# Attention and feed-forward in one kernel: value products and sums grouped on quarters of the array's columns, first transfers reordered

## The chip, the cores and the metric

The kernel runs on one core of one Trainium2 chip. A core has a matrix engine (TensorE, PE in the profile), three engines for elementwise work (VectorE, DVE; ScalarE, ACT; GpSimd, POOL) and a queue that issues transfers (SyncE, SP). The metric is the device time of one execution in microseconds. Comparisons use the median of several runs.

## The reference

Four batches of 448 tokens, 12 heads of 64. Attention with a soft cap, then a feed-forward block over all 1792 tokens (768 to 2048 to 768) with a squared ReLU:

```python
scores = q @ k.T / sqrt(64)
scores = cap * tanh(scores / cap)
attn = exp(scores - max(scores)); attn = attn / (sum(attn) + 1e-9)
x = (attn @ v)                      # heads side by side: [1792, 768]
h = x @ w_in                        # [1792, 2048]
g = s * max(h, 0) ** 2 + b
out = g @ w_out                     # [1792, 768]
```

The data have 64-bit inputs, which the kernel reads as pairs of 32-bit words and converts itself (weights: 512 KB per piece of 128 x 512).

## The kernel before, in words

**Attention.** The 12 heads of a batch are worked in 6 pairs (24 pairs in all). For a pair, `load` (L376) transfers keys, queries and values. `scores` (L387) makes the transposed scores in four calls: c = 0, 1, 2 take 128 keys each, and two matmuls, one per head, run beside each other on the two halves of the array's rows (L402); c = 3 takes the 64 keys that are left of both heads, in one matmul on the full array (L398). Each is fp32, which the chip runs as two passes, so a call of two matmuls stands in the trace as x4, and one as x2. ACT then applies tanh (L409) and exp (L413). The score PSUM has two buffers.

`pv` (L453) makes what comes after: `value(c)` multiplies the exps by the values, for c < 3 with one matmul per head on halves of the array's columns (L466), for c = 3 with one matmul on the full array (L462). `total` sums the exps over the keys by matmuls with ones, on quarters of the columns (L474): the first call takes c = 0 and 1, the second c = 2 and 3. Each of the six calls is an operation of its own for PE. The result (one PSUM buffer, `ps_v`) is copied to `pw` (L482 on ACT or L483 on DVE); the sums go through small transfers to be inverted and spread (`normal`, L417), POOL multiplies (`num`, L336), and after six pairs a batch is scaled and split into a high and a low fp16 half (`x`).

**Feed-forward.** `m1` (L711) makes one block of 128 of the 2048 columns for a batch: 18 fp16 matmuls (high x high, high x low, low x high; L722 to L724), then ReLU (L732), square (L737), high half (L325) and low half (L335 or L336) into `gt`. `m2` (L750) makes one block of 128 output columns: 48 fp16 matmuls (L768 to L770) in four operations of 12, then scaling (L788) and the transfer out. The weights are converted on the chip in `win` (L565) and `wout` (L628): sign and exponent work on DVE and POOL, squares for a norm (L579), then high and low halves.

**What sets the order.** Every operation is recorded in a `Plan` (L20) with a duration, a rank and what it reads and writes. `emit` (L67) simulates the engines: at each step every engine offers, of its operations in order of rank, the first that can start at once, or else the one that can start first, and the earliest of all is taken. The chip then runs exactly this order on each queue. `CHOICE` (L204) holds the ranks (`spans`), the engines that may take each kind of work, and the number of buffers. On SP, transfers without dependencies go out by rank: before, the ranks of the first weight piece, the scalars (-13 to -11) and the first keys and queries (-12) lie close together. Ahead of all stands a warm-up of 11 matmuls on zeros (L833).

Of the kernel before, what the change touches and what calls it, by code (L numbers as in the profile page):

```python
# [7 lines left out]
F32 = mybir.dt.float32  # L8
# [5 lines left out]
ALU = mybir.AluOpType  # L14
# [5 lines left out]
class Plan:  # L20
# [32 lines left out]
                found[k] = True  # L53
        return list(found)

    def op(self, eng, dur, rank, fn, r=(), w=(), move=0.0, port=False, late=0.0):
        self.any({eng: (dur, fn)}, rank, r, w, move, port, late)

    def any(self, ways, rank, r=(), w=(), move=0.0, port=False, late=0.0):

        self.ops.append((ways, rank, tuple(r), tuple(w), move))
        self.more.append((port, late))

    def emit(self):  # L67
        n = len(self.ops)
# [30 lines left out]
        busy = {}  # L99
# [9 lines left out]
        before = {"PE": 0.14, "POOL": 0.02}  # L109
        shy = CHOICE["shy"]  # L110
        cold = 0.0

        def when(i, eng):
            ways, _, r, w, _ = self.ops[i]
# [31 lines left out]
        while todo:  # L146
            best = None
            for reach in (80, n):
                for e, q in queue.items():
                    pick = None  # L150
                    for i in q[:reach]:
                        t = when(i, e)
                        if t is not None and (pick is None or t < pick[0] - 1e-6):
                            pick = (t, i)
                            if t <= busy[e]:
                                break
                    if pick and (best is None or pick[0] < best[0]):
# [12 lines left out]
            for k in self.base((*r, *w)):  # L170
                if k not in held:
                    p = self.make[k][0]
                    held.add(k)
                    slot[k] = head[p] % len(free[p])
                    free[p][slot[k]] = None
                    head[p] += 1
            if e == "PE":
                if t - busy[e] > 3.0:
                    cold = t + 4.0
                if t < cold:  # L180
                    dur += min(dur, (cold - t) / 2)
# [20 lines left out]


CHOICE = {  # L204
    'bias': 6,
    'shy': {'DVE': 0.3, 'POOL': 0.5},
    'spans': {
        ('a', 0): (-2.0, 64.9),
        'w': (-8.6, 102.1),
        ('m1', 0): (65.4, 102.7),  # L210
        'o': (97.1, 180.8),
        ('m2', 0): (93.5, 201.5),
        ('a', 1): (112.5, 186.2),
        ('m1', 1): (199.3, 288.6),
        ('m2', 1): (275.5, 309.7),
        ('a', 2): (151.1, 242.3),
        ('m1', 2): (111.6, 298.4),
        ('m2', 2): (278.3, 336.0),
        ('a', 3): (286.2, 308.4),
        ('m1', 3): (421.3, 519.9),  # L220
        ('m2', 3): (346.0, 349.0),
    },
    'alias': 2,
    'direct': 6,
    'cslag': 13,
    'late': 0.5,
    'warm': 11,
    'pvo': 0.52,
    'pair': 0.85,
    'evac': ('ACT', 'DVE'),  # L230
    'sq': ('ACT', 'DVE'),
    'expo': ('POOL',),
    'whi': ('DVE', 'POOL'),
    'ohi': ('DVE', 'POOL'),
    'xhi': ('ACT', 'DVE', 'POOL'),
    'xmul': ('POOL',),
    'relu': ('ACT', 'DVE'),
    'gsq': ('ACT', 'DVE'),
    'glo': ('DVE', 'POOL'),
    'ghi': ('ACT',),  # L240
    'cs': ('DVE', 'POOL'),
    'slots': (
        ('w', 7), ('kraw', 3), ('qraw', 3), ('vp', 3), ('t', 2), ('ph', 3), ('pt', 2), ('rd', 3), ('pw', 3),
        ('num', 11), ('cmp', 3), ('x', 6), ('r', 2), ('sq', 5), ('o', 2), ('cs', 2),
    ),
}

# [2 lines left out]
def attention_moe_kernel(  # L250
# [123 lines left out]


    def load(bb, c2, rank, vrank):  # L376
        kr = buf(("k", bb, c2), "kraw", [128, SK], F32)
        dma(262144, rank - 10, lambda: nc.sync.dma_start(P[kr], kT[bb, c2]), w=[kr])
        kq = buf(("q", bb, c2), "qraw", [128, S], F32)
        dma(229376, rank - 10, lambda: nc.sync.dma_start(P[kq], qT[bb, c2]), w=[kq])  # L380
        kv = buf(("v", bb, c2), "vp", [128, NC + 1, 2 * D], F32)
        dma(
            262144, vrank - 10,
            lambda: nc.sync.dma_start(P[kv].rearrange("p a d -> p (a d)"), v2[bb * NP + c2]), w=[kv],
        )

    def scores(bb, c2, c, rank):  # L387

        kr, kq = ("k", bb, c2), ("q", bb, c2)
        kp = buf(("sc", bb, c2, c), "ps_s", [128, 2, 512], F32)  # L390
        kt = buf(("t", bb, c2, c), "t", [128, 2, S], F32)
        last = c == NC
        kh = buf(("ph", bb, c2, c), "pt" if last else "ph", [128, S] if last else [128, 2, S], F32)

        def mm():
            ps, k, q = P[kp], P[kr][:, c * 128:(c + 1) * 128], P[kq]
            if last:
# [55 lines left out]
    def pv(bb, c2, rank, step):  # L453

        kv = ("v", bb, c2)
        kp = buf(("pv", bb, c2), "ps_v", [128, 2, 512], F32)
        kh = [("ph", bb, c2, c) for c in range(NC + 1)]

        def value(c):
# [8 lines left out]
        def total(first):  # L468
            for h in range(2):
                for i in range(2):  # L470
                    o = h * D + i * 32
                    w, c = (half[:, h], NC) if i and not first else (ones[:, 0:32], i if first else 2)
                    ph = P[kh[c]] if c == NC else P[kh[c]][:, h]
                    nc.tensor.matmul(P[kp][o:o + 32, 1, 0:S], w, ph, start=first, stop=not first)  # L474

        for c in range(NC + 1):
            pe(0.9, rank + c * step, lambda c=c: value(c), r=[kh[c], kv], w=[kp])
            if c % 2:
                pe(0.9, rank + c * step, lambda c=c: total(c == 1), r=[kh[c - 1], kh[c], "one"], w=[kp])
# [460 lines left out]
```

## Time and profile before

| | |
|---|---|
| timed runs, median of 3 | 687.01 us (686.17 to 689.37) |
| the profiled execution, its own time | 685.4 us |
| its span in the trace | 683.6 us |
| mean granted clock of TensorE | 0.998 |
| busy: PE / DVE / ACT / POOL | 671.0 / 308.8 / 328.7 / 151.8 us |
| matmuls in the trace | 3515 |

The page's busy times say how long each engine had work; for PE the ends of matmuls are modelled, since they are pipelined. The chain of waits follows the work that ended last back to the start; where it stays on one engine, each piece lasts until the next one on that engine starts, so that a piece's time is what this work cost there. The shapes `64*128`, `128*64`, `128*32` and `128*128` are rows by columns of the array that one matmul uses.

### The profile page before, as it was taken

The numbers are of one execution on the slowest core, as the hardware profiler recorded it, in microseconds if no ns is written. First come the engines' busy times: TensorE is split into PE (matmuls) and PEld (weight loads), VectorE is DVE, ScalarE is ACT, GpSimd is POOL, SyncE is SP. The second block draws the span as 40 slices with busy tenths as digits, with TensorE's granted clock in tenths as the row PEclk, the third lists the DMA queues.
The fourth block names the chain that finished last, engine by engine and source line by source line (L and its number), as shares of the span: only waits on it lengthen the run. The fifth ranks groups of instructions, "written<-read, shape, count | busy, mean of one in ns | idle before, by whom it ended". The sixth has DMA issues, their size and how long they took to land.

```text
span 683.6 us, 9313 instructions
## 1 busy us (share of the span) xinstructions
PE 671.0 (98%) x3515; PEld 294.3 (43%) x3515; DVE 308.8 (45%) x651; ACT 328.7 (48%) x451; POOL 151.8 (22%) x178
## 2 busy tenths in 40 slices
PE   7999989999999999999999999999999999999997
PEld 2223234455333334355545333335554555554553
DVE  3877789986989999943331011111111310111000
ACT  5987886646446544635532455354551103553100
POOL 1333344543655646610010000000000100000000
PEclk9999999999999999999999999999999999999999
DMA  8663763212576577570003333111001542000410
GB/s 287 242 209 104 251 199 125 93 59 93 153 241 202 158 253 246 147 271 1 1 32 119 120 119 118 57 47 45 1 1 38 202 142 85 0 1 32 123 55 27
DMA packets 43100, 80.29 MB, mean 117 GB/s; under 512 B 15408, under 2 KB 24624, under 8 KB 43056
## 3 DMA queue, kind: packets, MB, share of 16 engines
q1 hardware_dynamic: 43056, 79.71, 35.5%
q8 instruction: 27, 0.44, 0.3%
q14 instruction: 17, 0.14, 0.1%
HBM read 67.63 MB, written 11.88 MB: 116 GB/s over the span
## 4 chain that ended last, share of the span: by engine, by line
PE 87%; DVE 5%; DMA 3%; POOL 1%; issue 1%; ACT 0%; SPq 0%; POOLq 0%; ACTq 0%
PE ps_m L722 10%; PE ps_m L723 10%; PE ps_m L724 10%; PE ps_m L768 10%; PE ps_m L770 10%; PE ps_m L769 10%; PE ps_s L402 8%; PE ps_v L466 7%; PE ps_v L474 5%; PE ps_s L398 3%; PE ps_v L462 3%; DVE w L345 1%; DVE w L545 1%; DVE w L542 1%; POOL w L328 1%
## 5 line engine op out<-in xcount | busy, mean ns | idle before, releaser
L768 PE MATMUL ps_m<-gt,w 128*128 128x448 f16 x384 | 135.6, 353 | 1.0 <-ACT r L732 0.7
L722 PE MATMUL ps_m<-x,w 128*128 128x448 f16 x384 | 135.4, 352 | 0.0
L723 PE MATMUL ps_m<-x,w 128*128 128x448 f16 x384 | 135.3, 352 | 0.0
L770 PE MATMUL ps_m<-gt,w 128*128 128x448 f16 x384 | 135.3, 352 | 0.0
L724 PE MATMUL ps_m<-x,w 128*128 128x448 f16 x384 | 135.3, 352 | 0.0
L769 PE MATMUL ps_m<-gt,w 128*128 128x448 f16 x384 | 135.3, 352 | 0.0
L409 ACT ACTIVATE t<-ps_s,arena 128x896 f32<-128x896 f32 x96 | 85.9, 908 | 46.1 <-PE ps_s L402 31.8
L335 DVE TENSOR_TENSOR gt<-r,gt 128x448 f16<-128x448 f32 x54 | 34.8, 645 | 146.4 <-ACT gt L325 146.4
L732 ACT ACTIVATE r<-ps_m,arena 128x448 f32<-128x448 f32 x61 | 38.6, 633 | 117.6 <-PE ps_m L724 117.6
L788 ACT ACTIVATE o<-ps_m,arena 128x448 f32<-128x448 f32 x24 | 17.4, 724 | 149.0 <-PE ps_m L770 141.8
L413 ACT ACTIVATE ph<-t,par 128x896 f32<-128x896 f32 x72 | 74.1, 1039 | 12.4 <-PE ps_v L474 11.4
L336 POOL TENSOR_TENSOR num<-pw,rd 128x448 f32<-128x448 f32 x24 | 29.0, 1208 | 213.7 <-DMA rd<-zd 188.7
L402 PE MATMUL ps_s<-qraw,kraw 64*128 64x448 f32 x288 | 73.5, 595 | 2.1 <-DMA qraw<-in_qT 2.1
L466 PE MATMUL ps_v<-ph,vp 128*64 128x448 f32 x288 | 67.4, 560 | 1.9 <-ACT pw L482 1.4
L768 PEld LDWEIGHTS <-w 128*128 128x128 f16 x384 | 37.6, 98 | 48.0 <-issue 11.4
L722 PEld LDWEIGHTS <-w 128*128 128x128 f16 x384 | 37.8, 98 | 36.0 <-issue 1.5
L770 PEld LDWEIGHTS <-w 128*128 128x128 f16 x384 | 37.6, 98 | 35.1
L724 PEld LDWEIGHTS <-w 128*128 128x128 f16 x384 | 37.6, 98 | 35.0
L723 PEld LDWEIGHTS <-w 128*128 128x128 f16 x384 | 37.6, 98 | 34.9 <-issue 0.3
L769 PEld LDWEIGHTS <-w 128*128 128x128 f16 x384 | 37.6, 98 | 34.3 <-issue 1.3
L474 PE MATMUL ps_v<-ph,ones 128*32 128x448 f32 x288 | 45.9, 551 | 0.0
L328 POOL TENSOR_SCALAR w<-w,arena 128x256 f16<-128x256 f32 (+1 forms) x55 | 37.9, 708 | 27.9 <-DVE arena L610 17.6
(99 smaller groups left out, 665.0 us busy)
## 6 DMA issues: line engine op xcount, KB each, us to landing
w<-w SPq DMA_DIRECT2D x48, 512.0 KB, 4.0
w<-in_w_out SPq DMA_DIRECT2D x24, 512.0 KB, 5.3
w<-in_w_in SPq DMA_DIRECT2D x18, 512.0 KB, 5.9
kraw<-in_kT SPq DMA_DIRECT2D x24, 256.0 KB, 3.6
vp<-in_v SPq DMA_DIRECT2D x24, 256.0 KB, 3.5
qraw<-in_qT SPq DMA_DIRECT2D x24, 224.0 KB, 3.8
rd<-zd SPq DMA_DIRECT2D x48, 112.0 KB, 2.9
out_dram<-o SPq DMA_DIRECT2D x24, 224.0 KB, 3.2
```

The costliest lines, as they stand in the source:

```text
L328: 0.1 + n * 0.00107, lambda: nc.gpsimd.tensor_scalar(dst(), src(), sc, 1.0, ALU.mult, ALU.mult)
L402: nc.tensor.matmul(ps[:, h, 0:S], k[rows], q[rows], start=True, stop=True)
L409: lambda: nc.scalar.activation(P[kt][:, e], P[kp][:, e, 0:S], AF.Tanh, scale=tsc[:, 0:1]),
L413: 0.67 if last else 1.04, rank, lambda: nc.scalar.activation(ph(), P[kt][:, e], AF.Exp, scale=par[:, 0:1]),
L466: nc.tensor.matmul(out[o], v[:, o], P[kh[c]][:, h], start=(c == 0), stop=False)
L474: nc.tensor.matmul(P[kp][o:o + 32, 1, 0:S], w, ph, start=first, stop=not first)
L722: nc.tensor.matmul(ps[:, 0:S], wh, x[:, 0], start=(c == 0), stop=False)
L723: nc.tensor.matmul(ps[:, 0:S], wh, x[:, 1], start=False, stop=False)
L724: nc.tensor.matmul(ps[:, 0:S], wl, x[:, 0], start=False, stop=(c == NP - 1))
L768: nc.tensor.matmul(ps[:, 0:S], wh, ghi[:, f], start=(f == 0), stop=False)
L769: nc.tensor.matmul(ps[:, 0:S], wh, glo[:, f], start=False, stop=False)
L770: nc.tensor.matmul(ps[:, 0:S], wl, ghi[:, f], start=False, stop=(f == NF - 1))
```

## The change

Values run on the same quarters as the sums, and the six calls of a pair become two operations for PE: value 0, value 1 and the first sum; value 2, value 3 and the second sum. Each call is now four matmuls, one per quarter (two passes each). Each PE operation has a kind: 1 for scores on halves of the rows, 2 for values and sums, 0 for all others. The planner charges 0.19 us for a change of kind, and among the operations that PE can start at once prefers one of the same kind, if its rank lies within 0.34 of the first. The first pair's keys and queries get the rank -100, the scalars -89 to -87, so that these are the first five transfers. `CHOICE` gets other ranks, engines and buffers; the branch under `pre` is not used, since `pre` is empty.

```diff
-        self.more.append((port, late))
+        self.more.append((port, late, kind))
...
+                        if pick and pick[0] <= busy[e] and self.ops[i][1] > self.ops[pick[1]][1] + cling:
+                            break
                         t = when(i, e)
-                        if t is not None and (pick is None or t < pick[0] - 1e-6):
+                        if t is None:
+                            continue
+                        if pick and pick[0] <= busy[e]:
+                            if t <= busy[e] and self.more[i][2] == kind:
+                                pick = (t, i)
+                                break
+                        elif pick is None or t < pick[0] - 1e-6:
                             pick = (t, i)
-                            if t <= busy[e]:
+                            if t <= busy[e] and (e != "PE" or self.more[i][2] == kind):
                                 break
...
             if e == "PE":
+                if self.more[i][2] != kind:
+                    kind = self.more[i][2]
+                    dur += 0.19
...
-    'bias': 6,
+    'bias': 1.14,
...
-        ('a', 0): (-2.0, 64.9),
-        'w': (-8.6, 102.1),
-        ('m1', 0): (65.4, 102.7),
-        'o': (97.1, 180.8),
-        ('m2', 0): (93.5, 201.5),
-        ('a', 1): (112.5, 186.2),
-        ('m1', 1): (199.3, 288.6),
+        ('a', 0): (1.8, 65.3),
+        'w': (9.6, 136.9),
+        ('m1', 0): (77.0, 123.0),
+        'o': (113.5, 227.6),
+        ('m2', 0): (-9.8, 176.2),
+        ('a', 1): (127.9, 183.5),
+        ('m1', 1): (181.1, 233.4),
...
-    'cslag': 13,
+    'cslag': 21,
     'late': 0.5,
+    'cling': 0.34,
+    'parts': ((0, 1), (2, 3)),
+    'pre': (),
     'warm': 11,
-    'pvo': 0.52,
-    'pair': 0.85,
-    'evac': ('ACT', 'DVE'),
-    'sq': ('ACT', 'DVE'),
+    'pvo': 0.73,
+    'evac': ('ACT',),
+    'sq': ('ACT', 'DVE', 'POOL'),
     'expo': ('POOL',),
-    'whi': ('DVE', 'POOL'),
-    'ohi': ('DVE', 'POOL'),
-    'xhi': ('ACT', 'DVE', 'POOL'),
+    'whi': ('ACT', 'DVE'),
+    'ohi': ('POOL',),
+    'xhi': ('DVE',),
     'xmul': ('POOL',),
-    'relu': ('ACT', 'DVE'),
-    'gsq': ('ACT', 'DVE'),
-    'glo': ('DVE', 'POOL'),
-    'ghi': ('ACT',),
+    'relu': ('ACT',),
+    'gsq': ('ACT',),
+    'glo': ('POOL',),
+    'ghi': ('POOL',),
     'cs': ('DVE', 'POOL'),
...
-        ('w', 7), ('kraw', 3), ('qraw', 3), ('vp', 3), ('t', 2), ('ph', 3), ('pt', 2), ('rd', 3), ('pw', 3),
-        ('num', 11), ('cmp', 3), ('x', 6), ('r', 2), ('sq', 5), ('o', 2), ('cs', 2),
+        ('w', 7), ('kraw', 3), ('qraw', 3), ('vp', 3), ('t', 2), ('ph', 4), ('pt', 2), ('rd', 3), ('pw', 3),
+        ('num', 9), ('cmp', 3), ('x', 6), ('r', 2), ('sq', 5), ('o', 2), ('cs', 2), ('su', 1),
...
     def load(bb, c2, rank, vrank):
+        if bb == c2 == 0:
+            rank = -90
...
-        pe(0.85 if last else CHOICE["pair"], rank, mm, r=[kr, kq], w=[kp])
+        pe(0.75, rank, mm, r=[kr, kq], w=[kp], kind=0 if last else 1)
...
+        quarter = [(h, i, slice(h * D + i * 32, h * D + i * 32 + 32)) for h in range(2) for i in range(2)]
+        prob = lambda c, h: P[kh[c]] if c == NC else P[kh[c]][:, h]
 
         def value(c):
-            v, out = P[kv][:, c], P[kp][:, 0, 0:S]
-            if c == NC:
-                nc.tensor.matmul(out, v, P[kh[c]], start=False, stop=True)
-                return
-            for h in range(2):
-                o = slice(h * D, (h + 1) * D)
-                nc.tensor.matmul(out[o], v[:, o], P[kh[c]][:, h], start=(c == 0), stop=False)
...
+            for h, _, o in quarter:
+                nc.tensor.matmul(P[kp][o, 0, 0:S], P[kv][:, c, o], prob(c, h), start=(c == 0), stop=(c == NC))
...
+        for part in CHOICE["parts"]:
+            both = not pre and part[0] == 0
+
+            def run(part=part, both=both):
+                for c in part:
+                    value(c)
+                if both:
+                    total(True, False)
+                if not pre and part[-1] == NC:
+                    total(False, True)
+
+            n = len(part) + both + (not pre and part[-1] == NC)
+            pe(
+                0.75 * n, rank + part[-1] * step, run, r=[*(kh[c] for c in part), *(kh[0:2] if both else ()), kv, "one"],
+                w=[kp], kind=2,
+            )
...
     for i, a in enumerate((cap, s, b)):
-        dma(512, -13 + i, lambda i=i, a=a: nc.sync.dma_start(par[:, i:i + 1], a.to_broadcast([128, 1])), w=[("par", i)])
+        dma(512, -89 + i, lambda i=i, a=a: nc.sync.dma_start(par[:, i:i + 1], a.to_broadcast([128, 1])), w=[("par", i)])
```

The other ranks of `spans` change as well.

## Rows read from the trace of the kernel before

**Rows 1.** The page: busy us, share of the span, instructions of each engine

```profile
PE 671.0 (98%) x3515; PEld 294.3 (43%) x3515; DVE 308.8 (45%) x651; ACT 328.7 (48%) x451; POOL 151.8 (22%) x178
```

**Rows 2.** PE's own waits: waited for, us in total, times, longest

```profile
PE ps_s L402 <- DMA qraw<-in_qT: 2.1, 1, 2.1
...
PE ps_v L466 <- ACT pw L482: 1.4, 1, 1.4
```

**Rows 3.** The chain of waits over the span: start us, us, what

```profile
2.58 5.61 DMA qraw<-in_qT
8.33 3.98 PE ps_s L402 x12
12.31 1.20 PE ps_s L398 x2
13.51 1.65 PE ps_v L466 x8
15.16 0.89 PE ps_v L474 x8
...
17.00 0.90 PE ps_v L466 x4
...
67.81 1.70 PE ps_s L402 x8
...
451.68 0.95 PE ps_s L402 x4
...
461.03 0.90 PE ps_v L466 x4
461.93 0.95 PE ps_v L462 x2
520.77 0.89 PE ps_v L474 x8
```

**Rows 4.** The chain between 396 and 440 us

```profile
408.71 0.29 PE ps_m L768
```

**Rows 5.** Three stretches: busy us of each engine, granted clock, DMA

```profile
8.00:56.00 48.00, 47.67 (x245) 14.04 (x245) 34.05 (x64) 40.19 (x48) 15.28 (x17) 0.96 0.70 243
80.00:230.00 150.00, 146.74 (x800) 63.53 (x800) 129.08 (x262) 89.13 (x125) 75.95 (x85) 1.00 0.48 156
542.80:679.80 137.00, 136.27 (x720) 70.19 (x718) 17.16 (x36) 35.79 (x59) 1.54 (x2) 1.00 0.19 62
```

**Rows 6.** PE's groups by line: busy us, mean ns of one

```profile
L768 PE MATMUL ps_m<-gt,w 128*128 128x448 f16 x384 | 135.6, 353 | 1.0 <-ACT r L732 0.7 <-DVE arena L506 0.2
```

**Rows 7.** The chain in the last 8 us

```profile
679.61 0.20 PE ps_m L770
```

**Rows 8.** Order of time, first 9 us: start us, us, engine, line

```profile
0.73 0.39 SPq L533 DMA_DIRECT2D gt<-in_w_in  x1
...
2.05 4.16 PE L833 MATMUL ps_m<-w 128*128 128x448 f16 x11 [2.05 <-POOL w L836]
```

**Rows 9.** Transfers: issues, KB each, median us to landing

```profile
qraw<-in_qT SPq DMA_DIRECT2D x24, 224.0 KB, 3.8
```

**Rows 10.** ACT's groups by line: busy us, mean ns of one

```profile
L409 ACT ACTIVATE t<-ps_s,arena 128x896 f32<-128x896 f32 x96 | 85.9, 908 | 46.1 <-PE ps_s L402 31.8 <-PE ps_s L398 14.1
L413 ACT ACTIVATE ph<-t,par 128x896 f32<-128x896 f32 x72 | 74.1, 1039 | 12.4 <-PE ps_v L474 11.4
...
L413 ACT ACTIVATE pt<-t,par 128x448 f32<-128x448 f32 x24 | 16.0, 666 | 0.3
...
L482 ACT ACTIVATE pw<-ps_v 128x896 f32<-128x896 f32 x14 | 12.6, 903 | 1.0 <-PE ps_v L474 1.0
```

**Rows 11.** POOL's groups by line, shapes apart: busy us, mean ns of one

```profile
L328 POOL TENSOR_SCALAR w<-w 128x512 f32<-128x512 f32 x42 | 31.6, 754 | 46.6 <-DVE w L542 28.0 <-issue 4.1 <-DVE arena L506 3.2
L336 POOL TENSOR_TENSOR num<-pw,rd 128x448 f32<-128x448 f32 x24 | 29.0, 1208 | 213.7 <-DMA rd<-zd 188.7 <-ACT r L737 14.8 <-DVE w L542 5.0
L328 POOL TENSOR_SCALAR w<-w,arena 128x256 f16<-128x256 f32 x43 | 26.4, 635 | 10.2 <-DVE arena L686 9.3 <-DVE arena L781 0.8
L336 POOL TENSOR_TENSOR cs<-cs,w 128x512 f32<-128x512 f32 x12 | 17.0, 1418 | 6.2 <-DVE w L545 6.0
L336 POOL TENSOR_TENSOR gt<-r,gt 128x448 f16<-128x448 f32 x10 | 12.0, 1197 | 14.5 <-ACT gt L325 14.5
```

More of the change, by code (lines that the diff above doesn't have):

```diff
@@ L54, in base, with op, any @@
         return list(found)
-    def op(self, eng, dur, rank, fn, r=(), w=(), move=0.0, port=False, late=0.0):
-        self.any({eng: (dur, fn)}, rank, r, w, move, port, late)
-    def any(self, ways, rank, r=(), w=(), move=0.0, port=False, late=0.0):
+    def op(self, eng, dur, rank, fn, r=(), w=(), move=0.0, port=False, late=0.0, kind=0):
+        self.any({eng: (dur, fn)}, rank, r, w, move, port, late, kind)
+    def any(self, ways, rank, r=(), w=(), move=0.0, port=False, late=0.0, kind=0):
         self.ops.append((ways, rank, tuple(r), tuple(w), move))
-        self.more.append((port, late))
+        self.more.append((port, late, kind))
     def emit(self):
@@ L111, in emit @@
         cold = 0.0
+        kind = 0
+        cling = CHOICE["cling"]
         def when(i, eng):
@@ L204 @@
 CHOICE = {
-    'bias': 6,
+    'bias': 1.14,
     'shy': {'DVE': 0.3, 'POOL': 0.5},
     'spans': {
-        ('a', 0): (-2.0, 64.9),
-        'w': (-8.6, 102.1),
-        ('m1', 0): (65.4, 102.7),
-        'o': (97.1, 180.8),
-        ('m2', 0): (93.5, 201.5),
-        ('a', 1): (112.5, 186.2),
-        ('m1', 1): (199.3, 288.6),
[L215 to L221, printed above, removed]
+        ('a', 0): (1.8, 65.3),
[5 more added lines that the diff above has]
+        ('m1', 1): (181.1, 233.4),
+        ('m2', 1): (276.1, 309.8),
+        ('a', 2): (169.9, 271.3),
+        ('m1', 2): (196.2, 351.6),
+        ('m2', 2): (320.3, 332.8),
+        ('a', 3): (286.3, 308.1),
+        ('m1', 3): (349.1, 513.5),
+        ('m2', 3): (368.2, 371.6),
     },
@@ L224 @@
     'direct': 6,
-    'cslag': 13,
+    'cslag': 21,
     'late': 0.5,
+    'cling': 0.34,
+    'parts': ((0, 1), (2, 3)),
+    'pre': (),
     'warm': 11,
-    'pvo': 0.52,
-    'pair': 0.85,
-    'evac': ('ACT', 'DVE'),
-    'sq': ('ACT', 'DVE'),
+    'pvo': 0.73,
+    'evac': ('ACT',),
+    'sq': ('ACT', 'DVE', 'POOL'),
     'expo': ('POOL',),
-    'whi': ('DVE', 'POOL'),
-    'ohi': ('DVE', 'POOL'),
-    'xhi': ('ACT', 'DVE', 'POOL'),
+    'whi': ('ACT', 'DVE'),
+    'ohi': ('POOL',),
+    'xhi': ('DVE',),
     'xmul': ('POOL',),
-    'relu': ('ACT', 'DVE'),
-    'gsq': ('ACT', 'DVE'),
-    'glo': ('DVE', 'POOL'),
-    'ghi': ('ACT',),
+    'relu': ('ACT',),
+    'gsq': ('ACT',),
+    'glo': ('POOL',),
+    'ghi': ('POOL',),
     'cs': ('DVE', 'POOL'),
+    'add': ('DVE', 'POOL'),
     'slots': (
-        ('w', 7), ('kraw', 3), ('qraw', 3), ('vp', 3), ('t', 2), ('ph', 3), ('pt', 2), ('rd', 3), ('pw', 3),
-        ('num', 11), ('cmp', 3), ('x', 6), ('r', 2), ('sq', 5), ('o', 2), ('cs', 2),
+        ('w', 7), ('kraw', 3), ('qraw', 3), ('vp', 3), ('t', 2), ('ph', 4), ('pt', 2), ('rd', 3), ('pw', 3),
+        ('num', 9), ('cmp', 3), ('x', 6), ('r', 2), ('sq', 5), ('o', 2), ('cs', 2), ('su', 1),
     ),
@@ L457, in pv @@
         kh = [("ph", bb, c2, c) for c in range(NC + 1)]
+        pre = bb in CHOICE["pre"]
+        quarter = [(h, i, slice(h * D + i * 32, h * D + i * 32 + 32)) for h in range(2) for i in range(2)]
+        prob = lambda c, h: P[kh[c]] if c == NC else P[kh[c]][:, h]
         def value(c):
-            v, out = P[kv][:, c], P[kp][:, 0, 0:S]
-            if c == NC:
-                nc.tensor.matmul(out, v, P[kh[c]], start=False, stop=True)
-                return
-            for h in range(2):
-                o = slice(h * D, (h + 1) * D)
-                nc.tensor.matmul(out[o], v[:, o], P[kh[c]][:, h], start=(c == 0), stop=False)
@@ L468, in total @@
[L468 to L479, printed above, removed]
+            for h, _, o in quarter:
+                nc.tensor.matmul(P[kp][o, 0, 0:S], P[kv][:, c, o], prob(c, h), start=(c == 0), stop=(c == NC))
@@ new lines, in total @@
+        def total(first, last):
+            for h, i, o in quarter:
+                if i and last:
+                    w, ph = half[:, h], prob(NC, h)
+                else:
+                    w, ph = ones[:, 0:32], P[ks][:, h] if pre else prob(i if first else 2, h)
+                nc.tensor.matmul(P[kp][o, 1, 0:S], w, ph, start=first, stop=last)
+        if pre:
+            ks = buf(("su", bb, c2), "su", [128, 2, S], F32)
+            for c in range(1, NC):
+                first = (lambda: P[kh[0]]) if c == 1 else (lambda: P[ks])
+                binary(
+                    CHOICE["add"], 2 * S, rank + c * step, lambda: P[ks], first, lambda c=c: P[kh[c]], ALU.add,
+                    [kh[0], kh[c]], [ks],
+                )
@@ new lines, in pv @@
+        for part in CHOICE["parts"]:
[11 more added lines that the diff above has]
+                w=[kp], kind=2,
+            )
@@ L480, in pv @@
+        if pre:
+            pe(0.75, rank + (NC + 0.5) * step, lambda: total(True, True), r=[ks, kh[NC], "one"], w=[kp], kind=2)
         kw = buf(("pw", bb, c2), "pw", [128, 2, S], F32)
```

## The prediction, made before the change was run

> **What bounds the kernel now.** Start with the page's busy times [rows 1]: PE is busy 671.0 us of 683.6, no other engine passes 48%. PE's own waits say the same from the other side: the largest is 2.1 us for the first queries, the next that lies among the work 1.4 us [rows 2]. So PE does not stop, and the time is the sum of what PE does. Only three things can shorten it: less work, less loss between pieces of work, an earlier start.
>
> How much is loss? The chain of waits over the whole span shows PE's calls one by one [rows 3]. A single call of scores on halves of the rows (L402 x4) takes 0.95 us, one of values on halves of the columns (L466 x4) 0.90, one of sums on quarters (L474 x8) 0.89, one of scores or values on the full array (L398, L462 x2) 0.95. But two value calls in a row (L466 x8) take 1.65, and two score calls in a row (L402 x8) 1.70. The second call of the same shape costs 0.75. So each uninterrupted visit to a shape carries an extra 0.20 (L402, L398, L462), 0.15 (L466) or 0.14 (L474, if its call too is 0.75). Of the fp16 matmuls, the first after such a visit takes 0.29 [rows 4], a later one 0.189 (720 of them in 136.3 busy us at the end, [rows 5]): 0.11 extra, rounded up.
>
> I counted the visits by merging neighbouring matmuls of one shape over the whole trace; the first and the last of each kind stand in [rows 3]: 66 to L402, 60 to L466, 48 to L474, 47 to the full-array fp32 calls; and 27 to the fp16 matmuls of the feed-forward part. In time: 66 x 0.20 + 60 x 0.15 + 48 x 0.14 + 47 x 0.20 + 27 x 0.11 = 13.2 + 9.0 + 6.7 + 9.4 + 3.0 = 41.3 us.
>
> Check of the sum: fp16 2304 x 0.189 (six lines of 384, one of them in [rows 6]) = 435; attention 24 pairs x 10 calls x 0.75 = 180; start of the first score call 8.3 [rows 3]; 3.8 us of tail from the end of the last matmul [rows 7] to the span's end; visits 41.3. That is 668.4, and the span is 683.6. The missing 15 are 24 visits of one-column matmuls (L369, L591, L663, some 11 us with what they wait for) and about 4 us of short stalls, mostly in the first pair.
>
> **The change part by part.** *Values on quarters, in blocks.* All of a value call now runs as four matmuls on the same four column quarters as the sums, and the work is issued as two blocks per pair: value 0, value 1, first sum; value 2, value 3, second sum. The calls stay at six per pair, so the 0.75 each stay; what goes is visits. Before, those to L466, L474 and L462 (24 of the 47) were 132, 5.5 per pair, and cost 9.0 + 6.7 + 4.8 = 20.5 us. After, 48 blocks at 0.14 cost 6.7. Saved: 13.8.
>
> *Scores.* With 48 interruptions instead of 132, two score calls can oftener stand together (their PSUM has two buffers). At best 40 visits instead of 66, at worst all 72 alone: 8.0 to 14.4 us, against 13.2. I take 58: 11.6. The 24 last score calls (full array) cost 4.8 before; beside fp16 matmuls, which have their shape, about half: 2.4 to 4.8, I take 4.0. Against this, blocks and scores may cut the feed-forward matmuls oftener: 40 to 60 visits instead of 27, 4.4 to 6.6 us; I take 5.0. After: 6.7 + 11.6 + 4.0 + 5.0 = 27.3 us, so 14.0 saved; with the ends, 19.8 down to 8.8.
>
> *Price of a value call on quarters.* The trace has sums on quarters, each matmul with weights and a stream of its own, at 0.89 for a lone call, never two in a row: all 48 visits are x8 [rows 3]. So the second and third call of a block lie between 0.75 (as for halves) and 0.89 (if nothing of the entry is hidden): 96 calls x 0 to 0.14 = 0 to 13.4 us. I take 0.75, since L466, with 0.90 alone and 0.75 as second, differs only in its number of columns.
>
> The Trainium skill, in TensorE: Matmul & The Clock Gate (Part 3: Packing small matmuls), gives 2.38x as measured for three column tiles at once. An estimate by that page: a call on quarters is a quarter longer, 0.95 without its entry, and the 96 value calls would add some 19 us, which puts the time above before. The trace disagrees: 0.89 with its entry [rows 3].
>
> *First transfers.* Before, a weight piece goes out on SP at 0.73, then two scalars, then keys and queries; the queries are issued at 2.58 and take 5.61, and PE starts at 8.33 [rows 3], while the warm-up is over at 2.05 + 4.16 = 6.21 [rows 8]. Now keys and queries are first: issued at about 0.73 and 1.2, there at 5.0 with the median 3.8 us to landing [rows 9], at 6.8 with 5.61. PE starts at 6.2 to 7.0: saved 1.3 to 2.1, I take 2.1. The scalars go out half a microsecond or so later, hidden by the warm-up. The first weight piece moves from 0.73 to about 3, behind five issues of some 0.45. It feeds DVE, then the first fp16 matmuls, at 103 us; attention of the second batch covers it until then. Cover gone, it costs those 2.3.
>
> *A new wait.* A block waits for two exps where a value call waited for one, and holds what is behind it on PE's queue. ACT must keep pace: per pair its tanh and exp take (85.9 + 74.1 + 16.0) / 24 = 7.3 us and the copy, now always on ACT, 0.90 [rows 10]: 8.2. PE needs 7.5 + 2 x 0.14 + 3 x 0.20 = 8.4 per pair where attention runs alone, instead of 7.5 + 38.3 / 24 = 9.1. ACT was already busy 40.2 of 48.0 us there, with squares of weights among it [rows 5]. If it keeps those, at some 0.7 each, PE waits for ACT by 0 to 1.0 us per pair, over 7 pairs 0 to 7. I take 2.5. Later the fp16 matmuls fill such gaps.
>
> *New engines.* The high and low half of the squared activations move to POOL (from ACT and mostly DVE), weight splits from POOL to ACT and DVE. By POOL's nearest rows a high half takes 0.75, a low half 1.20 [rows 11]; 1.95 per feed-forward column is under PE's 18 x 0.189 = 3.4, so 0 is taken. At the change from one matmul phase to the next the last low half comes 0.7 us later or so; the first 36 matmuls of the next output column (6.8 us), which don't need it, cover that.
>
> Sum: -14.0 - 2.1 + 2.5 = -13.6. The profiled execution took 685.4 (span 683.6): 671.8 for it. The median of the timed runs, 687.0, lies 1.6 above; from there it is 673.4. I say 672.5, between the two.
>
> **The rivals.**
> *A: ACT paces the first stage.* Blocks start late, fewer score calls merge: 7 instead of 2.5 and 8.8 instead of 14.0. -8.8 - 2.1 + 7 = -3.9: 683. For it: ACT at 84% there. Against: only 1.4 us of PE's waits are for an ACT copy [rows 2], and POOL, idle for two thirds of that stage [rows 5], may now take the squares.
> *B: the further calls of a block cost 0.89*: -13.6 + 13.4, no change, 687. For it: no row has two such calls. Against: the second L466 call. (The skill's ratio would make it 692; its chance is in B's.)
> *C: slower, POOL becomes the bound in the weight stage.* From 80 to 230 us POOL was busy 76.0 of 150 [rows 5]. What may now fall there: 32 feed-forward columns x 1.95 = 62, conversion of output weights 24 x 0.75 = 18, their high halves 48 x 0.635 = 30, column sums 18 x 1.42 = 26, twelve products x 1.2 = 14 [rows 11]: 150 of 150. If contention lengthens these by a fifth, 30 us are left over, and PE, with product buffers cut from 11 to 9, cannot work ahead on pairs for long: -13.6 + 30, 703. It decides from about 165 us of POOL work in that stretch. Against: DVE may take the column sums, which takes 26 off, and part of the second batch may come later.
> *D: more is saved.* The good ends of the visits, no pacing: -19.8 - 2.1 = -21.9, 665.
>
> **How the numbers follow.** Forecast 0.62 (667 to 680), A 0.14, B 0.08, C 0.08, D 0.08. About 0.5% (3.4 us) is what a measurement here can tell from no change: under 683.6 is faster, over 690.4 slower. Faster: 0.62 + 0.08 + 0.10 of A + 0.03 of B and C = 0.83; slower: the long ends of B and C, 0.08; same 0.09. The range for 8 in 10, 662 to 684, holds forecast, most of D and A.
>
> **What would show it.** In the chain after: 48 blocks of 24 matmuls on quarters, 2.39 us each (2.67 would be B), no values on halves or on the full array; the fp32 visits down from 221 to some 120 to 140. First score call at 6.2 to 7.0. PE busy still 97% or more; if less, its list of waits names ACT's exps or copies before 75 us (A), or POOL's halves between 80 and 230 (C). I am wrong if the visits don't fall by 80 or more, or if they do and PE has over 10 us of new waits.

## The result and the profile after

The changed kernel took 676.07 us (median of four runs, 674.61 to 678.64), the kernel before 686.59 in runs beside it: ratio 0.9841, 95% interval 0.9803 to 0.9878. The profiled execution took 675.28 us against 685.4, with a span of 673.5 against 683.6. The forecast was 672.5, its range 662 to 684.

PE still sets the time, so the profile after is read for what PE loses. First the page: busy us, share and instructions of each engine, then the chain's shares by engine.

```profile
PE 657.4 (98%) x3947; PEld 300.4 (45%) x3947; DVE 288.2 (43%) x601; ACT 291.5 (43%) x390; POOL 247.2 (37%) x289
...
PE 61%; DVE 16%; DMA 11%; POOL 3%; issue 3%; ACT 3%; SPq 2%; DVEq 0%; POOLq 0%; ACTq 0%
```

and the chain's shares before:

```profile
PE 87%; DVE 5%; DMA 3%; POOL 1%; issue 1%; ACT 0%; SPq 0%; POOLq 0%; ACTq 0%
```

PE's busy time is 13.6 us less than in [rows 1], while the span is only 10.1 less. Before, PE held 87% of the chain and DVE 5%; now it is 61% and 16%. Where PE's work shrank, something else ends last more often.

The chain of waits over the whole span shows the blocks (start us, us, what; against [rows 3]):

```profile
65.16 1.64 PE ps_v L483 x16
66.80 0.75 PE ps_v L491 x8
...
67.86 1.70 PE ps_s L421 x8
...
89.98 0.95 PE ps_s L417 x2
```

A block of two value calls and a sum takes 1.64 + 0.75 = 2.39 us. A pair of score calls and a single call on the full array cost what they did before.

The order of time in the first 9 us (start us, us, engine, line) shows the start, SP's transfers and PE's first matmuls; [rows 8] are the lines of before:

```profile
0.73 0.39 SPq L397 DMA_DIRECT2D kraw<-in_kT  x1
1.18 0.42 SPq L399 DMA_DIRECT2D qraw<-in_qT  x1
...
3.54 0.43 SPq L572 DMA_DIRECT2D gt<-in_w_in  x1
```

```profile
2.05 4.29 PE L872 MATMUL ps_m<-w 128*128 128x448 f16 x11 [2.05 <-POOL w L875]
6.27 2.43 PE L421 MATMUL ps_s<-qraw,kraw 64*128 64x448 f32 x8
```

Scores start at 6.27 instead of 8.33, when the warm-up is over.

Merging neighbouring matmuls of one shape over PE's trace, as for the prediction, and taking each visit's time above its work gives this account of the two spans (us). A visit is an unbroken run of matmuls of one shape; "other losses" are what visits took beyond the usual cost of their shape, so waits within them and stretches at a lower clock:

| | before | after | difference |
|---|---|---|---|
| first score call | 8.3 | 6.3 | -2.1 |
| visits to a shape, fp32 count | 221 | 119 | |
| visits, cost above the work | 39.2 | 20.6 | -18.6 |
| one-column visits, with their waits | 10.9 | 12.0 | +1.1 |
| other losses of PE, first 104 us | 2.7 | 3.4 | +0.7 |
| other losses of PE, after 104 us | 1.5 | 9.3 | +7.8 |
| losses in the last visit (fp16), and the tail behind it | 5.1 | 6.2 | +1.1 |

Together -10.0 of the -10.1. The change saved more than the forecast said, and gave 10.7 us back, most of it between 104 and 312 us. (The tail from the end of the last matmul is 3.8 us in both. The last 1.1 is PE, in its last run of fp16 matmuls, standing twice instead of once for ACT's ReLU: `PE ps_m L807 <- ACT r L771` is 1.6 us in two waits, before it was 0.7 in one.) PE's own waits (waited for, us in total, times, longest), against [rows 2]:

```profile
PE ps_s L421 <- ACT t L428: 3.3, 3, 2.6
PE ps_m L702 <- DVE cs L352: 2.9, 2, 1.8
PE ps_m L872 <- POOL w L875: 2.1, 1, 2.1
```

The third is the warm-up's. The first, for tanhs, is new; the second, for a column sum's additions on DVE, was 1.0 us in one wait before. For 104 to 312 us the table of stretches (us, busy of PE, PEld, DVE, ACT, POOL with counts, granted clock, DMA share, GB/s) shows for the changed kernel:

```profile
104.00:178.00 74.00, 71.29 (x438) 34.24 (x437) 70.28 (x122) 42.39 (x62) 53.98 (x56) 0.98 0.36 114
104.00:312.00 208.00, 201.72 (x1287) 86.13 (x1287) 184.78 (x362) 113.39 (x146) 129.87 (x146) 0.98 0.50 163
249.99:253.40 3.41, 3.41 (x18) 0.64 (x20) 2.93 (x8) 2.95 (x4) 2.97 (x6) 0.50 0.16 25
```

and for the kernel before:

```profile
104.00:178.00 74.00, 74.00 (x413) 36.95 (x413) 62.18 (x124) 41.22 (x66) 37.14 (x38) 1.00 0.30 100
104.00:312.00 208.00, 206.90 (x1093) 89.60 (x1092) 173.56 (x358) 109.57 (x151) 106.35 (x118) 1.00 0.50 165
```

DVE is now busy 70.3 of the 74 us from 104 to 178, POOL 54.0. PE idles 6.3 us from 104 to 312, and in three stretches of 3.41 us (171.48, 249.99 and 308.02) the granted clock is 0.50, 1.2 instead of 2.4 GHz. Each follows a pause of PE; by the start of the visit in which PE stood, 2.8 us at 167.6, 1.3 at 244.5 with 0.5 at 249.6, 1.9 at 304.3. In those stretches a block took 3.50 and another 4.09 instead of 2.39, and the feed-forward matmuls lost 1.5 us: 4.3 us in all, on top of the pauses.

The waits around the first pause (engine line waited for: us, times, longest) name one behind the other:

```profile
...
ACT w L342 <- DVE arena L649: 4.2, 1, 4.2
...
PE ps_s L421 <- ACT t L428: 2.6, 1, 2.6
```

PE waits for a tanh. The tanh stands on ACT's queue behind two high halves of weight pieces and two exps; the first high half waits 4.2 us for its scale from DVE. From 158 us to that scale DVE is never idle for longer than 0.6 us. Its costliest groups over the whole span with shapes apart (busy us, mean ns) are

```profile
L581 DVE SCALAR_TENSOR_TENSOR w<-w 128x512 int32<-128x512 int32 x42 | 39.1, 930 | 1.4
L584 DVE SCALAR_TENSOR_TENSOR w<-w 128x512 int32<-128x512 int32 x42 | 36.5, 883 | 2.0 <-POOL w L345 2.0
...
L580 DVE TENSOR_SCALAR w<-w 128x512 int32<-128x512 int32 x42 | 28.7, 684 | 14.4 <-DMA w<-in_w_out 10.1 <-DMA w<-in_w_in 3.7
```

the conversion of the weight pieces from 64-bit input: shift, sign (L580, L581), join (L584). There are 48 pieces; six are converted in the buffer `gt` and stand in rows of their own.

DVE has no more operations in this stage than before. From 104 to 178 us it had 124 operations before and has 122 now, and over the span its busy time fell by 20.6 us. The same steps took longer. Before, in this window (busy us, mean ns):

```profile
L545 DVE SCALAR_TENSOR_TENSOR w<-w 128x512 int32<-128x512 int32 x13 | 10.1, 798 | 0.0
...
L541 DVE TENSOR_SCALAR w<-w 128x512 int32<-128x512 int32 x12 | 8.2, 685 | 0.4 <-DMA w<-in_w_out 0.4
```

and after:

```profile
L584 DVE SCALAR_TENSOR_TENSOR w<-w 128x512 int32<-128x512 int32 x12 | 11.9, 1006 | 0.0
...
L580 DVE TENSOR_SCALAR w<-w 128x512 int32<-128x512 int32 x11 | 9.6, 870 | 0.8 <-DMA w<-in_w_out 0.8
```

With the sign step (994 to 1048 ns) a piece's conversion went from 2.48 to 2.92 us; for twelve pieces that is some 5 of DVE's 8.1 us more, an estimate from these rows. The last section comes back to it.

### The profile page after: what moved, and what is told of

Same layout as the page of the kernel before. It is cut to its first block, busy times and chain, and to the rows that moved or that the text cites. A ratio compares the mean times of both kernels' runs of the same rounds, so it can differ in the third digit from the quotient of the medians.

```text
span 673.5 us, 10234 instructions
## 1 busy us (share of the span) xinstructions
PE 657.4 (98%) x3947; PEld 300.4 (45%) x3947; DVE 288.2 (43%) x601; ACT 291.5 (43%) x390; POOL 247.2 (37%) x289
## 4 chain that ended last, share of the span: by engine, by line
PE 61%; DVE 16%; DMA 11%; POOL 3%; issue 3%; ACT 3%; SPq 2%; DVEq 0%; POOLq 0%; ACTq 0%
PE ps_m L761 9%; PE ps_m L763 9%; PE ps_m L762 9%; PE ps_m L807 9%; PE ps_m L809 9%; PE ps_m L808 9%; PE ps_v L483 4%; DMA w<-in_w_out 3%; DVE w L362 3%; DMA w<-in_w_in 2%; PE ps_s L421 2%; DVE w L584 2%; DVE w L581 2%; DMA rd<-zd 2%; DVE arena L367 2%
## 5 line engine op out<-in xcount | busy, mean ns | idle before, releaser
L807 PE MATMUL ps_m<-gt,w 128*128 128x448 f16 x384 | 135.4, 353 | 1.6 <-ACT r L771 1.6
L345 POOL TENSOR_SCALAR gt<-r 128x448 f16<-128x448 f32 x64 | 40.4, 631 | 214.4 <-ACT r L776 214.2
L771 ACT ACTIVATE r<-ps_m,arena 128x448 f32<-128x448 f32 x64 | 40.5, 633 | 147.0 <-PE ps_m L763 147.0
L428 ACT ACTIVATE t<-ps_s,arena 128x896 f32<-128x896 f32 x96 | 83.5, 911 | 30.8 <-PE ps_s L421 29.3
L353 POOL TENSOR_TENSOR gt<-r,gt 128x448 f16<-128x448 f32 x64 | 69.9, 1093 | 4.4
L421 PE MATMUL ps_s<-qraw,kraw 64*128 64x448 f32 x288 | 68.2, 577 | 3.3 <-ACT t L428 3.3
L483 PE MATMUL ps_v<-ph,vp 128*32 128x448 f32 x576 | 66.6, 564 | 1.1 <-ACT pw L521 0.9
L345 POOL TENSOR_SCALAR w<-w 128x512 f32<-128x512 f32 x42 | 37.0, 881 | 64.3 <-DVE w L581 46.5
L807 PEld LDWEIGHTS <-w 128*128 128x128 f16 x384 | 37.6, 98 | 40.6 <-issue 3.1
```

The lines of the kernel that those rows point to most:

```text
L345: 0.1 + n * 0.00107, lambda: nc.gpsimd.tensor_scalar(dst(), src(), sc, 1.0, ALU.mult, ALU.mult)
L353: "POOL": (0.1 + n * 0.00225, lambda: nc.gpsimd.tensor_tensor(dst(), a(), c(), op)),
L483: nc.tensor.matmul(P[kp][o, 0, 0:S], P[kv][:, c, o], prob(c, h), start=(c == 0), stop=(c == NC))
L807: nc.tensor.matmul(ps[:, 0:S], wh, ghi[:, f], start=(f == 0), stop=False)
```

## The experiments

All ratios are to the kernel before, run beside. "Order held" means that the list of operations on each queue is the original's; otherwise the planner lays a new one.

**The kernel before with only its first transfers moved.**

```diff
+        if bb == c2 == 0:
+            rank = -90
-        dma(512, -13 + i, ...
+        dma(512, -89 + i, ...
```

> The kernel before with the new order of the first transfers alone (keys and queries of the first pair, then the scalars). Theory (time is the sum of what PE does, and it starts earlier): first score call at 6.3 us instead of 8.3, time 2 us under the kernel before, ratio about 0.997. Rival (the first weight piece, now some 2 us later, sets the first fp16 matmuls, so the head start is given back as a wait near 100 us): start at 6.3 too, but time unchanged within 0.5 us, with 2 us more of PE waits before 105 us.

Ratio 1.0281 (1.0237 to 1.0325): slower. The scores did start at 6.07 us, but the planner laid another order with 33.8 us of other losses; PE's waits (us in total, times, longest) begin with

```profile
PE ps_m L369 <- DVE arena L502: 13.3, 2, 11.5
```

So this shows nothing of the transfers' own price. It shows that a new rank at the start can upset an order hundreds of microseconds long.

**The changed kernel, order held, values back on halves and the full array inside the blocks.**

```diff
-            for h, _, o in quarter:
-                nc.tensor.matmul(P[kp][o, 0, 0:S], P[kv][:, c, o], prob(c, h), ...)
+            if c == NC:
+                nc.tensor.matmul(out, v, P[kh[c]], start=False, stop=True)
+                return
+            for h in range(2):
+                nc.tensor.matmul(out[o], v[:, o], P[kh[c]][:, h], ...)
```

> The changed kernel with the same two blocks per pair in the same order on every queue, but the values inside them on halves of the columns (and the last on the full array) as before, so that a block holds two or three shapes. Theory (each visit to a shape costs 0.14 to 0.20 us): the first block goes from 2.39 to 2.54 us, the second to about 2.74, 0.50 us per pair, 24 pairs: 12 us over the changed kernel, so about 688 and no better than the kernel before. Rival (the gain comes from the new ranks and engines, the shape of the values matters little): within 3 us of the changed kernel, about 676.

Ratio 0.9884 (0.9846 to 0.9923). Its chain shows a second block of a pair, then a first:

```profile
60.63 0.90 PE ps_v L488 x4
61.54 0.95 PE ps_v L484 x2
62.48 0.93 PE ps_v L496 x8
...
68.30 1.65 PE ps_v L488 x8
69.95 0.89 PE ps_v L496 x8
```

2.78 and 2.54 us instead of 2.39. Its visits cost 32.9 us against 20.6, 12.3 more, as worked out. Yet the span rose only 7.5 (681.0 against 673.5; 5.3 against the second profile of the changed kernel, below), and by the ratios of the timed runs, 0.9884 against 0.9841, the loss is only some 3 us, where 12 were expected. The other losses fell from 12.7 to 9.0, and the clock fell once from 104 us on, not three times. Shapes cost PE what was said. In time the quarters were worth 3 to 7.5 us in this order, since a slower PE waits less for others, and with halves the kernel was still faster than the one before.

**The blocks with the old ranks, engines and buffers.**

```diff
-    'sq': ('ACT', 'DVE', 'POOL'),
+    'sq': ('ACT', 'DVE'),
...
-    'glo': ('POOL',),
-    'ghi': ('POOL',),
+    'glo': ('DVE', 'POOL'),
+    'ghi': ('ACT',),
```

> The changed kernel with the ranks, engines and buffers of the kernel before; only blocks on quarters, kinds in the planner and the first transfers are new. Theory (blocks save visits, the new engines and ranks are not needed for that, and bring the new waits): fp32 visits at 120 to 150, time 666 to 674. Rival (ranks and engines must fit the blocks): visits fall as much, but PE waits over 15 us more for exps and copies, time 680 or above.

Ratio 1.0055 (1.0026 to 1.0085): all of the gain gone, though its visits cost only 22.4 us. Other losses were 25.8, first the copy that closes a pair:

```profile
PE ps_v L483 <- ACT pw L521: 5.6, 4, 1.9
```

So the ranks and engines, of which I had priced the engines at nothing, carry the result at least as much as the quarters do: the old ones with quarters gain nothing, the new ones with halves 1.2%.

**A wider margin before one-column matmuls** (the planner adds it to the readiness of what they read), since the first pause stands at one.

```diff
-    'late': 0.5,
+    'late': 3.0,
```

> The changed kernel with a margin of 3.0 instead of 0.5 us in the planner for the one-column matmuls that depend on DVE or POOL (norms, sums over lanes, column sums), so that PE meets them when their data are there. Theory (about 10 us of the saving were given back because these matmuls stand in PE's queue before their data, and the clock falls to half behind each such wait): PE's waits for column sums are gone, no or one fall of the clock between 100 and 320 us, time 5 to 9 us under the changed kernel, 667 to 671. Rival (the blocks' wait for two exps gives it back, ACT sets the pace): no change within 2 us, about 676, the same three falls of the clock. Second rival (the weights are the bound there, so each 2.5 us of margin delays what needs them): slower, 678 to 684.

Ratio 1.0017 (0.9985 to 1.005). The remedy fell: visits 19.9, but other losses 24.2 in the order that came of it.

**The changed kernel once more**, in the same runs as the next three.

> The changed kernel once more, unaltered, beside the kernels of this round, so that they can be compared on one chip: ratio to the kernel before 0.980 to 0.988, as measured first (0.984).

Ratio 0.9838 (0.9796 to 0.9881), span 675.7, visits 20.6 again, other losses 15.3 instead of 12.7. Between two executions of one kernel the losses differ by some 2.6 us.

**The kernel before, order held, only the five first transfers moved to the front of SP's queue.**

```diff
+        first = [("k", 0, 0), ("q", 0, 0), ("par", 0), ("par", 1), ("par", 2)]
+        early = [next(i for i in out if k in self.ops[i][3] and ran[i] == "SP") for k in first]
+        out = early + [i for i in out if i not in early]
```

> The kernel before with its order on every queue held as it was, but for the five first transfers (keys and queries of the first pair, three scalars), which are issued ahead of all others. Theory (the loss of 20 us in the earlier run came from the planner's new order of everything else, not from the transfers): first score call at 6.1 to 6.3 us, 2 us or a little more off the time, ratio 0.996 to 0.998. Rival (the later first weight piece costs what the early keys give): start at 6.3, ratio 1.000, new PE waits between 50 and 105 us. Rival (transfers of the first microseconds are what cost 20 us): ratio above 1.01.

Ratio 1.0069 (1.0035 to 1.0103): slower. Scores start at 6.27, but DVE's order of time reads

```profile
8.77 0.43 DVE L544 TENSOR_SCALAR gt<-gt 128x512 int32<-128x512 int32 x1 [8.77 <-DMA gt<-in_w_in]
9.24 0.69 DVE L545 SCALAR_TENSOR_TENSOR gt<-gt 128x512 int32<-128x512 int32 x1
9.84 0.16 DVE L812 RECIPROCAL arena<-par 128x1 f32<-128x1 f32 x1
```

and ACT's

```profile
11.42 0.68 ACT L582 ACTIVATE sq<-gt 128x512 bf16<-128x512 f32 x1 [5.30 <-DVE gt L548]
11.98 1.90 ACT L412 ACTIVATE t<-ps_s,arena 128x896 f32<-128x896 f32 x2
```

DVE stands to 8.77 for the first weight piece, now issued at 3.06, and the reciprocal that the first tanh scales with stands behind two steps of its conversion. That scale is there by 10.3. The tanh comes only at 11.98, since on ACT's queue the square of the same weight piece stands ahead of it and waits 5.3 us for the end of the conversion. PE's waits show

```profile
PE ps_s L405 <- ACT t L412: 4.4, 1, 4.4
```

with the granted clock at half from 10.9 to 17.8 (before: 9.4 to 12.8). The first sum starts at 18.8 instead of 15.1, 3.7 us later; the rest of the span's 7.2 us more lies further on, with one more stretch at half clock at 287. In the changed kernel the order was laid anew: the reciprocal is ahead of the conversion on DVE, no square is ahead of the tanh on ACT, and the first tanh starts at 8.01.

**The pauses taken one by one.** Three pieces of PE's work on one-column sums moved later; two weight halves on ACT moved later, past the tanh; both. All on the finished order of the changed kernel.

```diff
+        for key, past in CHOICE["postpone"]:
+            postpone(key, past)
+    'postpone': ((('ops', 3), 1), (('bps', 3), 4), (('bps', 5), 2)),              # sums
+    'postpone': ((('w1h', 7, 1), 4), (('w1h', 7, 0), 4)),                         # ACT
```

> The changed kernel with its order held, but two column-sum matmuls (fourth and sixth block of output weights) let the next PE operations by: the fourth four of them, the sixth two, and the fourth's sum over lanes lets one score call by. Theory (they stand in PE's queue ahead of their data, and the clock falls to half behind each wait): PE's waits of 1.2 and 1.8 us for the halving adds are gone, with them the falls of the clock at 250 and 308 us, 4 to 6 us off the changed kernel, ratio to the kernel before 0.976 to 0.978. Rival (ACT sets the pace there, PE only waits elsewhere): same time as the changed kernel within 1.5 us, new waits of PE for tanh or exp of the same length.

> The changed kernel with its order held, but two weight splits on ACT (last block of input weights, about 167 us) let the next four tanh and exp operations by. Theory (ACT stood 4.2 us in front of a split whose scale DVE had not made, PE then waited 2.6 us for a tanh and ran at half clock for 3.4 us): both gone, 3 to 4 us off the changed kernel, ratio to the kernel before 0.978 to 0.980. Rival (DVE is the bound of that stage, the 3 us come back as a wait for the weights behind it): same time within 1 us, a new PE wait between 170 and 200 us.

> The changed kernel with its order held, with both earlier moves: the two column sums and one sum over lanes behind later PE operations, and the two weight splits on ACT behind four tanh and exp operations. Theory now held (the weight conversion on DVE and POOL runs as late as PE lets it, and a wait taken away at one place comes back behind the next weights): 0 to 2 us off the changed kernel, ratio to the kernel before 0.981 to 0.984, PE waits of 12 us or more over 20 us in all left. Rival (the two moves were each too small to be seen, and add): ratio 0.974 to 0.978.

Ratios 0.9827 (0.979 to 0.9865), 0.9824 (0.9787 to 0.9862), 0.9808 (0.9773 to 0.9843): none can be told from the changed kernel's. Each pause went where it was moved away, and another came. With both moved, PE's waits are

```profile
PE ps_m L726 <- POOL cs L377: 3.0, 1, 3.0
...
PE ps_m L785 <- DVE arena L731: 1.9, 1, 1.9
```

with the warm-up's left out, and its other losses are 15.3. Moving single operations does not pay; something behind them is late.

**Less work for DVE, order held:** the second operation of the sign step left out for the 24 pieces of output weights, so that these lose their signs.

```diff
-            nc.vector.scalar_tensor_tensor(lo(), hi(), -0x80000000, lo(), ...)
+            if kr[0] != "or":
+                nc.vector.scalar_tensor_tensor(lo(), hi(), -0x80000000, lo(), ...)
```

> The changed kernel with its order held; for the output weights the second of the two DVE operations that bring over the sign is left out (24 operations of 0.93 us on average, so the signs are lost), which takes 22 us off DVE between 130 and 310 us. Theory (DVE's conversion of output weights is what PE waits for in that stage): PE's waits for column sums and weights there go from about 8 us to under 2 us, falls of the clock between 200 and 320 us are gone, 4 to 7 us off the changed kernel, ratio to the kernel before 0.974 to 0.978. Rival (PE waits there because of ACT and of the fixed order, DVE has slack): within 1.5 us of the changed kernel, 0.982 to 0.986.

Ratio 0.9673 (0.9641 to 0.9704), span 664.1. Some 24 x 0.93 = 22 us of DVE's time went, and PE's other losses fell from 12.7 to 4.1. The stretch:

```profile
104.00:312.00 208.00, 206.22 (x1350) 89.57 (x1349) 169.02 (x349) 118.86 (x152) 135.75 (x150) 1.00 0.55 174
```

PE is busy 206.2 of 208 us at a granted clock of 1.00, with POOL busier than in the changed kernel. DVE's conversion of the weights, not POOL's own load, held this order back.

**Other ranks and engines**, chosen so that in the planner's own reckoning PE stands still less.

```diff
-    'bias': 1.14,
+    'bias': 9.92,
-    'evac': ('ACT',),
+    'evac': ('ACT', 'DVE'),
...
```

> The changed kernel with other ranks and engines (column sums and last conversions earlier, the copy on ACT or DVE, the high half on ACT or POOL, conversion steps on ACT or POOL, preference for the same kind up to 8.5 in rank), chosen so that in the planner's own reckoning PE stands still less. Theory (blocks are worth their 18 us if the order leaves no waits): visits cost about as much as in the changed kernel, PE's other losses from 13 to about 6 us, 5 to 8 us off the changed kernel, ratio 0.972 to 0.977. Rival (the planner's reckoning does not hold at this size, waits appear elsewhere): ratio 0.980 to 1.000.

Ratio 0.9859 (0.9824 to 0.9893), span 680.0. Here DVE has time,

```profile
104.00:312.00 208.00, 199.60 (x1278) 85.35 (x1271) 161.67 (x348) 131.15 (x176) 93.61 (x102) 0.98 0.47 152
```

and still PE's other losses are 24.4, at other places (2.8 at 17.2, 4.1 at 111.8, 2.5 at 218.8). So a DVE with time to spare is not enough; the order must fit too.

**A shorter sign step for all 48 pieces, order held:** one operation instead of two.

```diff
-            nc.vector.tensor_scalar(lo(), lo(), 29, None, ALU.logical_shift_right)
-            nc.vector.scalar_tensor_tensor(lo(), hi(), -0x80000000, lo(), ...)
+            nc.vector.tensor_scalar(lo(), hi(), -0x80000000, None, ALU.bitwise_and)
```

> The changed kernel with its order held, and one DVE operation fewer for every piece of the weights, input and output: the sign alone is taken over from the high word (one tensor_scalar), the three lowest bits of the fp32 significand, which came from the low word, stay zero, so weights keep 21 significant bits instead of 24. It takes 42 operations of 0.93 us and leaves the cheaper one, about 39 us off DVE. Theory (DVE's conversion is what PE waits for, in the stage of the output weights above all): as without the signs or a little better, waits of PE under 5 us without those of the first pair, no fall of the clock before the end, ratio to the kernel before 0.964 to 0.969. Rival (it was something else in that kernel, as the operands without signs): ratio 0.980 to 0.986.

665.61 us, ratio 0.9676 (0.9643 to 0.9708). It beats both kernels, by giving up the three low bits that come from the low word. The largest of PE's waits that are left (the second is the warm-up's), and its page:

```profile
PE ps_s L421 <- ACT t L428: 2.1, 3, 1.3
PE ps_m L871 <- POOL w L874: 2.1, 1, 2.1
PE ps_m L806 <- ACT r L770: 1.6, 2, 0.8
```

```profile
PE 651.3 (98%) x3947; PEld 299.4 (45%) x3947; DVE 242.7 (37%) x553; ACT 292.1 (44%) x390; POOL 240.4 (36%) x289
```

Other losses 3.7, visits 20.6. DVE is busy 45.5 us less than in the changed kernel, twice the 22 of the experiment with 24 pieces (48 steps of some 0.95 us; the expectation counted 42), and the second half brings no more: there DVE no longer holds up anyone who holds up PE.

## Why the prediction was right, and where it was not

**Visits: right, larger.** The forecast had 27.3 us left of 41.3. At its own prices the trace after has 48 x 0.20 (scores on halves) + 47 x 0.14 (blocks) + 24 x 0.20 (last scores) + 16 x 0.11 (fp16) = 22.8, so 18.5 saved instead of 14.0, inside the ends of 8.8 and 19.8. Against the forecast: fp16 visits 3.2 lower (16, where I took 40 to 60), scores 2.0 lower (48 visits, not 58), the last scores 0.8 higher. I had blocks and scores cut the feed-forward matmuls oftener; they came one behind the other and cut them less often than before. The experiment with halves, whose visits are 12.3 us dearer in the same order, shows the price of a visit directly. It also shows what the sum left out: time saved in visits came back in part as waits, so that the 12.3 were worth 3 to 7.5 us.

**A call on quarters: right.** 2.39 us per block was the forecast, 2.67 would have been rival B. By an estimate from the ratio that the Trainium skill gives (TensorE: Matmul & The Clock Gate, Part 3: Packing small matmuls), each call would have been about a quarter longer. The trace after does not show that either, with 1.64 for two value calls and 0.75 for the third call.

**First transfers: right in size, wrong in reasoning.** 2.06 us earlier, forecast 2.1. But "attention of the second batch covers" the weight piece is refuted for the old order: with the five transfers alone, the piece's conversion stood ahead of the tanh's scale on DVE's queue and its square ahead of the tanh on ACT's, and the time rose by 0.7%. The step looked at who needs the piece last, the fp16 matmuls, not at what is queued behind the engines that wait for it. In the changed kernel it came together with a new order for both.

**ACT's pace: not above the forecast.** 2.5 us was the forecast. All short losses of PE in the first 104 us rose by 0.7; since some 1.5 of those before belong to the first scores at half clock (9.4 to 12.8 us, [rows 3]), which is gone, the new ones may be up to 2.2. ACT was busy here

```profile
8.00:56.00 48.00, 47.35 (x354) 14.94 (x354) 35.07 (x65) 43.58 (x53) 17.99 (x17) 1.00 0.75 256
```

43.6 of 48.0 us, more than in [rows 5], and PE 47.4. Rival A did not come.

**New engines: wrong.** This is the step that failed: "1.95 per feed-forward column is under PE's 18 x 0.189 = 3.4, so 0 is taken." Behind 104 us PE lost 7.8 us more than before, and 1.1 more at one-column matmuls. I asked whether POOL could keep up with the work it was given. It could: 89.9 of 150 us from 80 to 230. What was not asked was who feeds ACT, which now takes weight splits, and whether DVE has room: it had 62.2 busy of 74 us before, and came to 70.3 with two operations fewer. The experiment that relieves DVE alone removes 8.6 us of the losses. Whether the engines, the ranks or PE's new pace filled DVE is not shown: they changed together. Rival C had the right stretch and the wrong engine: DVE, not POOL, and 7.8 us, not 30; POOL's part is at most that DVE's steps take longer beside it.

**The sum.** -18.6 - 2.1 + 0.7 + 7.8 + 1.1 + 1.1 = -10.0, forecast -13.6: two errors of opposite sign, 4.6 us more saved in visits and 10.7 given back where 2.5 was allowed, left a miss of 3.6 us; that it is so small is in part luck. The test named in the prediction, over 10 us of new waits, was met if all of PE's new losses count, 10.7 us, and not if only waiting does: 4.3 of these are slow clock, and the profile's list of PE's own waits grew from 8.6 to 11.9.

**What stays open.** That DVE's conversion holds back this order is shown. Whether another order with the full conversion would reach 664 us is not: the three new orders of the blocks (old choice, wider margin, other ranks) lost 24 to 26 us at places of their own, and postponing single operations only moved the pauses.

## What to carry to other kernels

When an engine without stops is made faster, price what feeds it at its new pace, along the queues of every engine between, in the stage where they are fullest; a share of busy time over the whole span (DVE 45%) hid a stage at 84%. Before moving a transfer, look at what stands behind its readers, on the queue of each engine that waits for it. Savings and waits do not add up freely: price a saving with the order held. In a kernel with a planned order, an edit of one rank is an edit of everything: change one thing with the order held, or the comparison tells nothing.

## What the hardware showed

In the changed kernel three pauses of PE behind 104 us were paid twice: 6.5 us of standing at 167.6, 244.5 to 249.6 and 304.3, then 4.3 us through the three stretches at a granted clock of 0.50. Not every wait is: the two of 0.78 us for the ReLU, at 511.9 and 621.8, were followed by no such stretch. With DVE relieved there was none from 104 to 312.

A tiny operation can take the time of a large one. In the order of time at the first pause, one line for DVE and one for POOL (start us, us, line):

```profile
164.16 1.29 DVE L378 TENSOR_SCALAR arena<-arena 128x2 int32<-128x2 int32 x1
```

```profile
164.13 1.28 POOL L353 TENSOR_TENSOR cs<-cs,w 128x512 f32<-128x512 f32 x1 [0.63 <-DVE arena L645]
```

The DVE operation on two elements per partition, 0.17 us as the median of its line, ended with POOL's addition, which had started 0.03 us before it; it is one of the steps to the scale that ACT waits for. The Trainium skill, SBUF — State Buffer, Who interferes with whom, says that DVE in a two-port mode, which a tensor_scalar can enter, contends with GpSimd for a shared pair of ports, and that the one that comes second is blocked for the other's whole instruction. The trace agrees here: the two ended 0.04 us apart.

The large steps show it too. In the changed kernel's trace, shift, sign and join of a piece take 0.43, 0.69 and 0.69 us (medians) where no POOL instruction runs beside them, and 0.78, 1.02 and 1.05 us where POOL is busy for nine tenths of the step or more. Handing work from DVE to POOL therefore does not free DVE by as much as its own busy time says; how much of the 7.8 us came this way, no run here isolates.
